# Eight early tiles of attention turned by TensorE in half precision instead of by DMA transposes, with a new issue order

## The chip, the cores and the metric

The kernel runs on one NeuronCore of a Trainium2 chip. A core has TensorE (PE, matrix products, writes to PSUM), VectorE (DVE), ScalarE (ACT), GpSimd (POOL) and SyncE (SP), each with a queue of its own that it works off in order, and 16 DMA engines that the queues feed; here SyncE issues all transfers. The metric is the device time of one execution in microseconds (us).

## The reference

```python
def _attn_ref(q, k, v, centroids):           # q, k, v: (4, 8, 768, 64); centroids: (8, 16, 64)
    q_assign = np.argmax(np.einsum('bhsd,hcd->bhsc', q_n, c_n), axis=-1)
    k_assign = np.argmax(np.einsum('bhsd,hcd->bhsc', k_n, c_n), axis=-1)
    mask = q_assign[:, :, :, None] == k_assign[:, :, None, :]
    scores = scale * np.matmul(q, k.transpose(0, 1, 3, 2))
    scores = np.where(mask, scores, -1000000000.0)
    attn = np.exp(scores - np.max(scores, axis=-1, keepdims=True))
    attn = attn / (np.sum(attn, axis=-1, keepdims=True) + 1e-09)
    return np.matmul(attn, v)

def _moe_ref(x, w1, w2, w3, w_out):          # x: (3072, 512); w1..w3: (512, 768); w_out: (768, 512)
    h = np.maximum(np.maximum(x @ w1, x @ w2), x @ w3)
    return h @ w_out
```

`q_n`, `k_n` and `c_n` are the rows divided by their norms. The output of attention, heads side by side, is the `x` of the feed-forward part. All inputs and outputs are float32. The kernel works with pairs of float16 numbers, a high half and a low half (the rest that the high half leaves), so that a product of two such numbers is three float16 products.

## The kernel before

**Tiles and stages.** There are 4 batches and 4 pairs of heads. A tile is 128 query rows of one head against all 768 keys. Each tile is a *step*; there are 192 steps, 48 to a batch. Three steps of each head of a pair (six steps) make a visit, and the visits go through a batch in two halves: the first three query blocks of all four pairs, then the last three. After 24 steps one half of a batch is complete, and its feed-forward part (`ffn`) can start: 18 groups of hidden products (`hid`, L1413) and three groups of output products (`outp`, L1468).

**A step** (`tile_units`): the score product (`pe`, L1256 and L1258, four matmuls into one of three `big` PSUM buffers), the row minimum with scaling on VectorE (`mx`, L1267), the exponential on ScalarE (`exp`, L1273), and then the tile is split into two float16 halves and turned so that keys lie on partitions, into `pt`. For batches after the first the tile is also divided by its row sums. There are two ways to turn it before the change. In steps 0, 2, 4 to 38 (`BY_PE`) TensorE transposes the float32 tile in six 128 x 128 blocks into a second `big` buffer (`ptr`, L1304), and the split happens on the way out of PSUM: the high half as a copy (L378 on ScalarE), the low half as a difference on VectorE (L1312). In all other steps the tile is split in SBUF: `hi` (a float16 copy, on ScalarE, GpSimd or VectorE), `lo` (the difference, L1279, on GpSimd or VectorE), both into `hl`; and one DMA transpose on SyncE's queue (`tr`, L1282) turns both halves at once into `pt`. Six turned tiles feed the product with the values (`av`, L1207, 36 matmuls).

**Preparation.** `prep` loads and splits the queries and keys of a pair and finds the clusters (among it L782 and L791, the cluster products of the first batch, and L548, a half-precision transpose of six blocks with its take L555), `v_prep` the values, `weights` the four weight matrices in pieces (`piece`: load, cast, L1030; `split16`: scale, high half, low half).

**What sets the order.** Every operation or short group is a unit of a plan; `ORDER` is a list of unit numbers written out in the source, and the units are issued in exactly that order, each to the queue of its engine. Where a unit may run on several engines, `HANDS` has a letter for it (V, S, G, Q for VectorE, ScalarE, GpSimd, SyncE). So the order of each engine's queue is fixed in the source. PSUM holds three `big` buffers (two banks each) and two `one` buffers (one bank each); the score tiles, the f32 transposes and the value products all share the three `big` ones, in the order of issue.

The names that matter below: `BY_PE`, `BY_16` (empty before the change), `hl`, `pt`, `big`, `HANDS`, `ORDER`, and `tile_units` with `ptr16` and `take16`, which stand in the source already but are used by no step before the change:

```python
        if step not in BY_16:
            u_t.append(add("SP", 1.43, tr, [u], [hl, pt], step, work=2.2))
            return
        o = big()
        def ptr16():
            d = o().bitcast(F16)
            for c in range(2 * QT):
                x = hl()[:, c // QT, c % QT * P : (c % QT + 1) * P]
                nc.tensor.transpose(d[:, c * P : (c + 1) * P], x, identh)
...
        u = add("PE", 0.85, ptr16, [u], [hl, o], step)
        for a in range(2):
            u_t.append(add({"ACT": 0.69, "DVE": 0.46}, 0, take16(a), [u], [o, pt], step))
```

Of the kernel before, what the change touches and what calls it, by code (L numbers as in the profile page):

```python
# [27 lines left out]
1 0 18 19 51 52 173 445 151 2-5 7 6 54 53 8-15 20 21 30 22-24 39 25 26 40 27 55 28 16 31 33 36 35 56 41 57 63  # L28
# [31 lines left out]
391-393 2645 1285 440 2646 2705 1289 1278 2638 1293 394 399 398 1290 463 2639 1301 467 441 1254 2647 2706 494  # L60
# [4 lines left out]
1296 534 507 1341 1297-1299 2650 480 536 509 1325 570 510 1355 508 1372 1356 512 537 1357 1300 1331 1332 513  # L65
# [5 lines left out]
2825 558 559 2674 1419 1402 1403 560 1404 1409 1434 2677 2676 1410-1412 2678 561 1420 562 487 1413 2765 1421  # L71
563-565 554 555 1396 628 1371 556 583 1405 566 1388 569 567 568 1426 2681 2683 1427 1414 577 2682 2679 1422
# [4 lines left out]
1507 1479 1470 1497 2699 1498 1508 1492 1483 1509 1460 2700 2702-2704 1510 1493 1461 1499 1511 1494 1462 1484  # L77
# [7 lines left out]
1602 1618 1610 1603 1625 2729 601 633 1626 2730 1611 605-607 2733 1633 1642 2735 2731 1619 1627 1628 1634 1643  # L85
# [1449 lines left out]
```

## Time and profile before

| | |
|---|---|
| median of 3 runs | 710.59 us (707.4 to 712.21) |
| profiled execution, time | 711.06 us |
| profiled execution, span from first to last instruction | 709.1 us |
| mean granted TensorE clock | 0.978 |
| DMA moved | 121.03 MB in 297795 packets, mean 171 GB/s |
| DMA transposes | 172, median 4.1 us from issue to landing |

The profile is one execution of the program on the chip. A row of a group gives line, engine, operation, output and inputs with their shapes, the count, then busy time and mean length in ns, then how long the engine stood idle just before these instructions and what ended that idle time. A row of the table by stages gives start and end of the stage, its length, and for each engine the busy time and, in brackets, the number of instructions; then the granted clock of TensorE as a share of full speed, the mean busy share of the 16 DMA engines and the rate. A row of the timeline gives start, length, engine, line, operation. Rows marked PEld are weight loads of TensorE, which overlap its products. The ends of matmuls are modelled.

### The profile page before, as it was taken

What the parts mean: (1) busy time and instruction counts of PE and PEld (TensorE: products, weight loads), DVE (VectorE), ACT (ScalarE), POOL (GpSimd) and SP (SyncE); (2) the same over time, 40 slices, a digit from 0 to 9 for tenths busy, and PEclk for the clock granted to TensorE, in tenths of its full rate; (3) what the DMA queues carried; (4) which work ended last, traced back from release to release, by engine and by line L of the source; (5) the groups of instructions that cost most, each with busy time, mean ns of one, the idle gap of its engine ahead of it and who ended that gap; (6) DMA issues with size and microseconds to landing.
All of it is one profiled execution on the core that took longest, in us unless ns stands there. A gap on an engine that the chain in (4) does not pass through costs nothing. (4 is left out here: it accounts for less than half of the span.)

```text
span 709.1 us, 13176 instructions
## 1 busy us (share of the span) xinstructions
PE 665.5 (94%) x4505; PEld 389.9 (55%) x4505; DVE 599.0 (84%) x1470; ACT 483.6 (68%) x841; POOL 403.3 (57%) x374
## 2 busy tenths in 40 slices
PE   3778778998999999999999999999999999999997
PEld 1554545555456655565555555655555646564663
DVE  7998999999998878999989888999899967784231
ACT  6988989989865657787767647786667775651000
POOL 3677887888656564857566545666584551531000
PEclk8578999999999999999999999999999999999999
DMA  6698878779798879998979998999999785775001
GB/s 225 199 216 182 207 210 205 188 174 202 168 196 188 172 126 217 197 185 195 215 156 194 179 189 181 185 196 196 197 194 178 145 164 112 148 158 125 1 1 60
DMA packets 297795, 121.03 MB, mean 171 GB/s; under 512 B 273024, under 2 KB 284160, under 8 KB 297728
## 3 DMA queue, kind: packets, MB, share of 16 engines
q1 hardware_dynamic: 297728, 120.20, 80.0%
q8 instruction: 35, 0.57, 0.3%
q14 instruction: 32, 0.26, 0.1%
HBM read 31.49 MB, written 6.29 MB: 53 GB/s over the span
## 5 line engine op out<-in xcount | busy, mean ns | idle before, releaser
L1267 DVE TENSOR_SCALAR_CACHE_REDUCE big<-big,nsc 128x768 f32<-128x768 f32 x192 | 192.7, 1016 | 11.4 <-PE big L1258 10.8
L1413 PE MATMUL one<-x,w16a 128*128 128x384 f16 x1152 | 197.0, 326 | 0.2
L1279 POOL TENSOR_TENSOR hl<-e,hl 128x768 f16<-128x768 f32 x86 | 144.4, 1682 | 61.1 <-ACT hl L378 34.2
L1413 PEld LDWEIGHTS <-w16a 128*128 128x128 f16 x1152 | 111.5, 98 | 75.7 <-issue 2.9
L1273 ACT ACTIVATE e<-big,nm 128x768 f32<-128x768 f32 x116 | 104.4, 901 | 49.7 <-DVE big L1267 32.3
L1256 PE MATMUL big<-qk 128*128 128x512 f16 (+1 forms) x384 | 96.6, 334 | 12.2 <-ACT e L1273 9.4
L1207 PE MATMUL big<-pt,v 128*64 128x384 f16 x1152 | 101.8, 330 | 2.4 <-ACT e L1273 1.4
L1413 PE MATMUL one<-x,w16b 128*128 128x384 f16 x576 | 98.9, 326 | 1.0 <-DVE worow L1098 1.0
L1258 PE MATMUL big<-qk 96*128 96x512 f16 (+1 forms) x384 | 96.1, 331 | 0.1
L1273 ACT ACTIVATE big<-big,nm 128x768 f32<-128x768 f32 x76 | 66.3, 872 | 43.7 <-DVE big L1267 35.3
L1207 PEld LDWEIGHTS <-v 128*64 128x64 f16 x1152 | 70.0, 111 | 33.2 <-issue 9.8
L1413 PEld LDWEIGHTS <-w16b 128*128 128x128 f16 x576 | 55.7, 98 | 40.1 <-issue 3.4
L1332 DVE SCALAR_TENSOR_TENSOR hl<-big,rs,hl 128x768 f16<-128x768 f32 x72 | 72.7, 1011 | 4.6 <-ACT hl L380 3.6
L380 ACT ACTIVATE hl<-big,rs 128x768 f16<-128x768 f32 x62 | 55.7, 898 | 27.3 <-issue 10.7
L1323 POOL TENSOR_SCALAR e<-e,rs 128x768 f32<-128x768 f32 x37 | 34.0, 919 | 65.9 <-DVE rs L1294 47.1
L1256 PEld LDWEIGHTS <-qk 128*128 128x128 f16 x384 | 35.3, 99 | 43.7 <-issue 22.1
L378 ACT CAST hl<-e 128x768 f16<-128x768 f32 x60 | 49.8, 831 | 5.3 <-POOL e L1323 4.5
L1258 PEld LDWEIGHTS <-qk 96*128 96x128 f16 x384 | 38.2, 100 | 27.1 <-issue 2.6
L818 POOL TENSOR_TENSOR qk<-stage,qk 128x768 f16<-128x768 f32 x26 | 43.8, 1686 | 9.2 <-ACT qk L378 5.5
L1468 PE MATMUL one<-wo,vf_h 128*128 128x512 f16 x216 | 48.3, 379 | 0.5 <-ACT o L380 0.4
L1468 PE MATMUL one<-wo,wf_h 128*128 128x512 f16 x216 | 48.3, 379 | 0.0
L1427 DVE SCALAR_TENSOR_TENSOR wf_h<-one,wf_h 128x384 f32<-128x384 f32 x48 | 26.5, 553 | 20.2 <-PE one L1413 19.6
(203 smaller groups left out, 1002.0 us busy)
## 6 DMA issues: line engine op xcount, KB each, us to landing
stage<-in_qk_dram SPq DMA_DIRECT2D x32, 384.0 KB, 4.3
wd<-in_moe_w_dram SPq DMA_DIRECT2D x18, 512.0 KB, 4.2
out_dram<-o SPq DMA_DIRECT2D x24, 256.0 KB, 2.9
qk<-qk SPq DMA_DIRECT2D x15, 384.0 KB, 4.3
qk<-qk SPq DMA_DIRECT2D x30, 192.0 KB, 3.5
stage<-in_v_dram SPq DMA_DIRECT2D x12, 384.0 KB, 4.0
wd<-in_moe_w_out_dram SPq DMA_DIRECT2D x6, 512.0 KB, 3.8
qk<-cl_t SPq DMA_DIRECT2D x60, 48.0 KB, 2.3
```

Source lines behind the costliest of these rows:

```text
L378: eng.copy(out, x)
L380: eng.activation(out, x, AF.Copy, scale=k)
L818: eng.tensor_tensor(t()[:, AQ, i], x(), t()[:, BQ, i], op=ALU.subtract)
L1207: nc.tensor.matmul(t()[D * i : D * i + D, 0:nb], v()[:, i, kt, a], pts[i % len(pts)]()[:, rows[i], c * QT + kt, :], start=(m == 0), stop=( ...
L1256: nc.tensor.matmul(t()[:, lo:hi], aq[:, qs], ak[:, lo:hi], start=True, stop=False)
L1258: nc.tensor.matmul(t()[:, lo:hi], bq[0:K2, qs], bk[0:K2, lo:hi], start=False, stop=True)
L1267: nc.vector.tensor_scalar(s, s, -SCALE if exact else nscs[:, b, pr : pr + 1], 3.0e38, op0=ALU.mult, op1=ALU.min, accum_out=nm())
L1273: nc.scalar.activation(e(), t()[:, 0:S], AF.Exp, bias=nm(), scale=-1.0, accum_out=r)
L1279: eng.tensor_tensor(hl()[:, 1, :], e(), hl()[:, 0, :], op=ALU.subtract)
L1332: eng.scalar_tensor_tensor(hl()[:, 1, :], e(), r(), hl()[:, 0, :], op0=ALU.mult, op1=ALU.subtract)
L1413: nc.tensor.matmul(t()[:, 0:nb], w16[jt // JA][:, jt % JA, wa, i, ct], x16[b, gi, ct]()[:, xa, 0:nb], start=(m == 0), stop=(m == 3 * CT - 1),)
L1468: nc.tensor.matmul(t()[:, 0:DM], h16(jt)[:, ha, tt * P : (tt + 1) * P], wo16[0][:, jt, wa, :], start=(m == 0), stop=(m == 3 * JT - 1),)
```

## The change

`BY_16` becomes the steps 1, 3, 5, 7, 9, 11, 13 and 15. These eight tiles are split in SBUF as before, and then TensorE transposes the two halves in twelve float16 blocks of 128 x 128 into a `big` PSUM buffer (seen there as float16), and two copies, one per half, take them to `pt`, each on ScalarE or VectorE. The DMA transposes of these steps fall away. With the steps 0, 2, 4 to 38, which went over TensorE before, the first 17 steps now need no DMA transpose. The plan has 3093 units instead of 3077 (eight times one TensorE unit and two takes more, one transfer less), so all numbers after the first such step shift, and `ORDER` and `HANDS` are replaced as a whole. No other line changes; line numbers after the order rise by one.

```diff
 ORDER = """
-1 0 18 19 51 52 173 445 151 2-5 7 6 54 53 8-15 20 21 30 22-24 39 25 26 40 27 55 28 16 31 33 36 35 56 41 57 63
...
+1 0 18 19 173 52 51 153 176 151 2-5 7 174 6 8-15 20 21 30 22 23 175 24 39 25 40 26 41 27 42 28 54 16 53 33 31
...
 HANDS = """
-VVSSSSSSVVSSSSSSGSGSGGQQGVSSGSGSVGQQGVSSSSGSSGQQGVSGGSVGSSGSSGGSGVSSGSSGSSGSSGVGSGSSGVSGSGGVVSGSGGSGGGGGVSGGSS
...
+VVSSSSVSVVVSSSSSGSGSGGQQGVSSSGGSGGQQGVVSGSGSGGQQGSGSGSSGSGGSGGGGGVSSGGGGSSGGGSVGSGVSGVGGSSGVSSGGGGSGGSSSVSSGSG
...
-    BY_16 = set()
+    BY_16 = set(range(1, 16, 2))
```

Counted over the whole order, VectorE has 1279 units instead of 1272, ScalarE 619 as before, GpSimd 348 instead of 339, TensorE 483 instead of 475 and SyncE 364 instead of 372. Of the sixteen takes eight are ScalarE's and eight VectorE's.

More of the change, by code (lines that the diff above doesn't have):

```diff
@@ L27 @@
 ORDER = """
-1 0 18 19 51 52 173 445 151 2-5 7 6 54 53 8-15 20 21 30 22-24 39 25 26 40 27 55 28 16 31 33 36 35 56 41 57 63
[31 rows of a table removed]
-391-393 2645 1285 440 2646 2705 1289 1278 2638 1293 394 399 398 1290 463 2639 1301 467 441 1254 2647 2706 494
[4 rows of a table removed]
-1296 534 507 1341 1297-1299 2650 480 536 509 1325 570 510 1355 508 1372 1356 512 537 1357 1300 1331 1332 513
[5 rows of a table removed]
-2825 558 559 2674 1419 1402 1403 560 1404 1409 1434 2677 2676 1410-1412 2678 561 1420 562 487 1413 2765 1421
-563-565 554 555 1396 628 1371 556 583 1405 566 1388 569 567 568 1426 2681 2683 1427 1414 577 2682 2679 1422
[4 rows of a table removed]
@@ L77 @@
-1507 1479 1470 1497 2699 1498 1508 1492 1483 1509 1460 2700 2702-2704 1510 1493 1461 1499 1511 1494 1462 1484
[7 rows of a table removed]
-1602 1618 1610 1603 1625 2729 601 633 1626 2730 1611 605-607 2733 1633 1642 2735 2731 1619 1627 1628 1634 1643
[8 rows of a table removed]
-1695 1723 1733 691 712 1741 2762 2763 619 1734 713 714 620 684 1742 2764 2768 1735-1737 1724 1725 695 621 1738
[12 rows of a table removed]
-1869 1870 2812 2946 1904 1839 1896 1871 1905 1872 1897 1873 1840 2814 1898-1900 1882 1891 1874 1912 2817 1913
-1914 2818 1906 1901 1929 2819 2821 1920 2815 1915 1916 1930 1917 1918 1907 1931-1933 1908 2816 2820 2822 1921
[10 rows of a table removed]
@@ L119 @@
-2071 2078 2859 2079 817 2091 2861 792 2092 818 819 2100 2080 820-822 2072 2860 793 2093 859 2862 2053 856 2064
[11 rows of a table removed]
-2900 893 2230 848 2231 2225 2237 2902 2245 918 913 914 2212-2214 877 2198 936 2215 2226 2905 2253 2907 2238
[11 rows of a table removed]
-945 2407 2396 3007 2367 2388 2950 2377 2368 2397 2408 2400-2402 3067 2409 2410 2952 2411 2415 2423 2424 2416
-2425 2954 2443 2412 2403 2417 2426 2404 2418 2419 2427 2413 2428 2420 2444 2445 2955 2378 2435 2379 2429 2421
-2380 2430 2446 2447 2436 2448 2437 2452 2957 2959 2469 2405 2422 2431 2414 2453 2438-2441 2470 2958 2471 2454
[9 rows of a table removed]
@@ L155 @@
-3010 3015 2596 3017 3019 3018 3020 3021 3025 3022-3024 3026 3027 3029 3028 3033 3030 3031 3034 3032 3035 3037
-3036 3041 3038-3040 3042 3043 3045 3044 3046-3049 3051 3050 3052 3053 3057 3054 3058 3055 3056 3059 3061 3060
-3062-3064 3068 3071 3069 3070 3016 3074 3072 3073 3075 3076
+1 0 18 19 173 52 51 153 176 151 2-5 7 174 6 8-15 20 21 30 22 23 175 24 39 25 40 26 41 27 42 28 54 16 53 33 31
[5 rows of a table added]
+182 981 1007-1009 166 142 201 993 1002 988 1003 982 183 184 1004 989 990 1013 1019 1010 185 1014 1015 126 1020
[10 rows of a table added]
@@ new lines @@
+230 1155 1136 1161 1156-1158 245 1137 246 1167 1162 247 231 1138 232 1163 248 1152 251 1171 1185 1168 233 249
[18 rows of a table added]
+1271 1351 1337 1343 531 1332 502 1272 1344 506 503 1338 1352 1310 532 473-475 2667 1296 535 466 1324 1333 478
[10 rows of a table added]
+569 628 1432 567 556 568 566 1441 583 1449 2842 1468 2706 1461 1469 1462-1464 1455 1465 2708 1470 1471 1423
+1456 1457 1424 1472 1473 1479 2709 1487 2713 1504 1474 1480 1488 1481 1489 1466 1458 1475 2669 2710 1490 1482
+1483 1491 1492 2711 1484 1505 1493 1485 2714 1506 2712 1494 2717 1496 1521 1507 1522 1497 1523 1498 1495 1486
@@ new lines @@
+1513 2715 1514 2716 1508 2718 1476 1515 2719 2720 1499 1509 1524-1526 1500 1516 1501 1502 1527 1510 1477 1528
+1511 1478 1517-1519 2724 1533 1541 1550 579 1534 1542 2725 1535 1543 1536 1551 1537 1544 1545 2783 1503 1512
[10 rows of a table added]
+680 1678 1679 1696 1639 1680 1688 1697 1681 1640 681-683 1698 1699 2762 685 1689 686 2763 2764 687 1690 1665
+604 616 708 617 1674 1682 1691 2767 1703 1712 2765 1704 1700 1705 688 2766 689 1701 1713 1714 1720 646 684
+1721 1706 650 1707 2768 1715 1716 690 651 1722 1717 2773 1737 2769 1729 1723 709 1724 652 653 710 1718 654-656
[9 rows of a table added]
@@ new lines @@
+1842 706 693 704 1810 694 707 705 735 732 1800 757 736 2809 758 759 763-765 729 740 1843 2810 1845 2811 1857
[3 rows of a table added]
+2820 2822 1891 1899 2827 2825 1900 1871 1892 1901 1893 2823 1872 1902 1903 1883 1894-1896 1884 1897 1904 2826
[8 rows of a table added]
+2032 2024 2013 2014 2037 2045 771 2858 2025 2038 2046 2033 2047 2048 2039-2041 2859 772 2061 2053 773-775 2054
[6 rows of a table added]
+2121 2883 825 2122 862 2135 2885 2127 2136 2113 2137 2886 2138 2128 863-865 2129 2130 2139 2131 801 798 2106
+799 800 797 2114 902 2123 2132 2884 2140 2141 2152 2887 2144 2889 2153 866 2133 2145 829 2154 2146 868 869 871
@@ L158 @@
+2142 872 2888 833 834 2147 2148 802 2890 2149 2891 2161 2895 2893 2169 870 803 2162 2155-2157 2894 2163 835
[3 rows of a table added]
+879 2194 2187 2201 880 2202 2203 2908 2177 2906 875 832 2188 2206 2215 2910 2207 2216 2217 2208 881-883 2218
[15 rows of a table added]
+2384 2413 2424 2425 2417 3083 2418 2419 2426 2427 2431 2439-2441 2970 2459 2432 2420 2968 2442 2433 2443 2434
[12 rows of a table added]
+3059 3061 3060 3062-3065 3067 3066 3068 3069 3073 3070-3072 3074 3075 3077 3076 3078-3080 3084 3087 3085 3032
+3090 3088 3089 3086 3091 3092
 """
 HANDS = """
-VVSSSSSSVVSSSSSSGSGSGGQQGVSSGSGSVGQQGVSSSSGSSGQQGVSGGSVGSSGSSGGSGVSSGSSGSSGSSGVGSGSSGVSGSGGVVSGSGGSGGGGGVSGGSS
@@ L162 @@
-GSSVSGSVSSGSSGSSGSGSVSSGGGGSSGGSSGSSSGSSGGSSGGGSSGGGSGSVSGGSSGQQGGVGSVSSSSGGGGQQGGVGSGSSVGGSSVQQGGVGSGSSGVGSSG
-QQVGVSGGSVGSGGSGQQVGVSGGVSSSGSVGQQGGVSSGVSGGGSSGQQGVVSSGSSSVGGGVQQGGVSSGSSGSGGSVQQVGVGSGSVSSGVSGQQVGVSSVSSGSGG
-SGQQGGVSSGSSGGGGSVQQGGVGSGSVGSGGSSGSGGSVGSSGSVGSSGSVGSSGSGGSSGSSGSSGSSVSSGSSGSSGSSGSSGSSGSSVSSGSSGSSGSSGSVSGSG
-GSVSVSVSGSVSGSVGSVSSGSVGGGSVSSGVSVSSGSVVSGSVGSGVSVSSGSVSVGSVGGVVSVGGGSVGSGSVGSGSSVGGGSVGSGSVSSGSVVGSVSVGGGSVSS
-GSSVGSGSVSGGVVSSGSSVSSGSVSGGSVGGGSSVVSGVVGVGSVSSGSSVGSGSVSSGSVGSGVSVGSGSVGSGVVSGGSSVVVGSVGGVSVGGGSVVGVGVVGSGSV
@@ L167 @@
-SGGVSVGGGSVGSGSVGSGVSVSGGSVSSGSVSSVSSVSGGSVSSGSVGVGSSVGSGSVGSGSVSGGSSVVSGSVGSGSVSGGSSVGGGSVSSGSVSSVSVVGVGSVGSG
-SVSSGSSVGSGSVSVGSVGSVSVVGGGSVGVGVVGSGVSVSSGSVGSGSVSVGVVVSGGSVSSGSVSGVSSVVVGSVVSGVVVSGSVVSVVVVGGSVVGGSVSVVVGVSV
-VSGSVVSGSVVVGVVVGGVVVVVSVSSVVVGSVVSGSVVSGSVVSGSVVVGSVVSGSSSVVVGGVVVSGVVVSGSVVSGSVVGGVVVGVSSVVVVSGSVVGGSVVGGVVV
-VGSVVSGSVVVVVSSVVVGGSVVGGSVVVGSVVGVSVVVVVVVGGSSSSVVSVSVVVVVVVSGSVVVVVVVVGSVVGVVVVVVVSVVVVSGVVVSVVVVGVSVVVVSVVV
-VVSS
+VVSSSSVSVVVSSSSSGSGSGGQQGVSSSGGSGGQQGVVSGSGSGGQQGSGSGSSGSGGSGGGGGVSSGGGGSSGGGSVGSGVSGVGGSSGVSSGGGGSGGSSSVSSGSG
@@ new lines @@
+GGSGGSSVSSGSSGSSGSSGVSGGGSGSSGGSGGSSSGGVGGSVSGSSSGSSGGSSSSVVSGQQVGVSSGSSSSGSGGQQGGVSSGSSGSGGSGQQGGVVSGSVGVGGSG
+QQGGVVGVSSGSGGSVQQGGVGVGSSGSGSVGQQGGVSSGVSGSGSSGQQGGVSVVSSGVGGVGQQVGVSGVSSGGGGSVQQGGVSGGSSSSGVSGQQGGVGGGVSSSGG
+SGQQGGVSVGVSGGGGSVQQGVVVSGSSGSSSGGSVSSGSSSSGSGGVSSSGVVSSVVVSSVVSGSVSSGVSSSGSSGVSGSSGSSGSGGVSGSSGVSGSSGSSGSSGSS
+GSSGSSGSSGSVSGSSGSVSVSVVGSVVGVGGVVSSGSVGSGSVSSGSSVSGGSVSSVVVVGGSSVSGGSVVGVVVGSGSSVGSVVVVSGVVSSGSSVGGVSVGVGVVGS
+GSSVGGGSVGGGSVSSGSSVSSGSVGVGSVSSVSSVGSGSVSSGSVSGGSSVSGGSVSSGSVSGGSSVSGGSVSSGSVGSGVSVGVGSVGSGSVGGVVSVGGGSVSVGSV
@@ L172 @@
+SSGSVVGSGVVGSGSVGSGSSVGGGSVGSGSVSGGVSVGGGSVSSGSVGGGSSVGGGSVSGGSVVSGSSVGSGSVGSGSVSSGSSVSSGSVGSGSVGSGSSVGGGSVSSG
+VVSGVSVVGSGVVSSGSVSSGSSVVGGVVSSGSVSSGSVVGSGSVVSGVVGGGSSVSSGVVVSGSVVGGSVVSSVVVSGGVVSGGSSVVSGVVVSGSVVSGSVVSGSVVS
+GSVVGGSSSSVVSGSVVVGSVVGGSVVVGSVVSGVVVSGSVSVVVGGSVVSGSVVGGSVVGGSVVGGVVVVGSSSSVVSVSVVSGVVVSGSVVGVSVVSGSVVGVVVSVV
+VSGSVVSGVVVSGSVVSGSVVSGSVVVVSSSSVVVGVVVGGVVVSGSVVSGSVVGGVVVGGSVSSVVSGSVVSVVVVSVSVVGVSVVGVVVVGGVSVSVVVGSVVVVVVV
+GVVVVVVSVVVVVVVVVVSS
 """
```

221 rows, old and new, of the table ORDER are left out of this document.

## The prediction, made before the changed kernel was run

> **What bounds the kernel now.** I read the head of the page first (span and busy shares), then the table by stages, then the groups and waits of one stage.
>
> ```profile
> span 709.1 us, 13176 instructions
> PE 665.5 (94%) x4505; PEld 389.9 (55%) x4505; DVE 599.0 (84%) x1470; ACT 483.6 (68%) x841; POOL 403.3 (57%) x374
> ...
> core 0: us, PE busy (x) PEld busy (x) DVE busy (x) ACT busy (x) POOL busy (x), PEclk, DMA share, GB/s
> 0.00:20.00 20.00, 6.77 (x25) 3.01 (x25) 15.51 (x48) 13.98 (x22) 6.81 (x38) 0.82 0.70 242
> 20.00:40.00 20.00, 16.86 (x88) 12.44 (x87) 19.64 (x44) 19.32 (x31) 13.78 (x11) 0.67 0.75 183
> 40.00:60.00 20.00, 16.44 (x101) 9.87 (x101) 16.84 (x35) 15.89 (x29) 15.72 (x11) 0.74 0.96 211
> 60.00:80.00 20.00, 15.66 (x132) 10.35 (x129) 18.83 (x39) 17.94 (x35) 16.03 (x14) 1.00 0.91 191
> 80.00:100.00 20.00, 13.14 (x105) 8.56 (x106) 19.54 (x36) 18.96 (x37) 17.32 (x15) 1.00 0.81 218
> 100.00:200.00 100.00, 92.91 (x679) 55.64 (x676) 98.00 (x238) 88.41 (x161) 78.58 (x72) 1.00 0.80 188
> 200.00:640.00 440.00, 438.50 (x2990) 254.51 (x2989) 389.72 (x999) 302.28 (x520) 252.26 (x213) 1.00 0.90 178
> ```
>
> The table splits the run in two. From 200 to 640 us TensorE (PE) is busy 438.50 of 440 us: there the time is TensorE's work and nothing else, and VectorE (DVE), ScalarE (ACT) and GpSimd (POOL) have room. Before 200 us it is the other way round. TensorE idles 13.23 us in the first 20 and 25.0 in the 180 after (3.14 + 3.56 + 4.34 + 6.86 + 7.09), while VectorE idles there 0.36 + 3.16 + 1.17 + 0.46 + 2.00 = 7.15 us. So the change, whose tiles all lie ahead of 100 us, works in the one part that TensorE does not fill, and the engine that has nothing to spare there is VectorE. ScalarE is next (18.96 of 20 at 80 to 100), GpSimd has most room, the DMA share is at its highest from 40 to 80 us.
>
> ```profile
> L1267 DVE TENSOR_SCALAR_CACHE_REDUCE big<-big,nsc 128x768 f32<-128x768 f32 x30 | 30.0, 1016 | 1.8 <-PE big L1258 1.6
> L1256 PE MATMUL big<-qk 128*128 128x512 f16 x64 | 18.3, 373 | 8.5 <-ACT e L1273 7.4 <-DVE pt L1312 0.8 <-DVE xs L1226 0.2
> L1304 PE MATMUL big<-ident,e 128*128 128x128 f32 x84 | 13.9, 309 | 4.7 <-ACT e L1273 3.7 <-DVE pt L1312 0.8
> ...
> L1279 POOL TENSOR_TENSOR hl<-e,hl 128x768 f16<-128x768 f32 x13 | 23.2, 1789 | 9.2 <-DVE hl L382 3.7 <-ACT hl L378 2.7 <-issue 1.9
> ```
>
> These are groups from 25 to 105 us. The score product (L1256) waits 7.4 us for the exponential of an earlier tile, which frees one of the three `big` PSUM buffers; the f32 transposes (L1304) wait 3.7 us for the exponential that makes their input. Neither waits for a transfer. L1279 is the split of a tile into its low half, most often on GpSimd.
>
> **The change part by part.** *Transfers taken away.* Eight of the 172 DMA transposes go, those of steps 1, 3 to 15.
>
> ```profile
> L1282 SPq DMA_TRANSPOSE pt<-hl x172: 1274/1561/3469, 35.1 to 648.3; - x172
> ...
> who waited for it (us, times):
>   POOL hl L382: 1.4, 2
>   ACT hl L378: 0.2, 1
> ```
>
> SyncE's queue loses 8 x 1.561 = 12.5 us of issuing, so loads queued behind them go out sooner. But in the whole run the engines waited only 1.4 + 0.2 = 1.6 us for these transfers. The gain is thus between 0 and 1.6 us by that row; I take 0 here, since both waits are GpSimd's and ScalarE's, and carry the relief of the DMA share as an unknown below.
>
> *TensorE.* Each tile now gets twelve 128 x 128 transposes in half precision. The trace has the same operation in L548, six blocks at once, once at the granted half clock and once at full:
>
> ```profile
> 33.54 0.82 PE L548 MATMUL one<-identh,cl_t 128*128 128x128 f16 x6 [1.69 <-DVE cl_t L543]
> ...
> 60.50 0.50 PE L548 MATMUL one<-identh,cl_t 128*128 128x128 f16 x6
> L548 PE MATMUL one<-identh,cl_t x12: 217/254/314, 33.5 to 60.8; 128*128 128x128 f16 x12
> ```
>
> At full clock six take 0.50 us, of which 0.25 is one block's length, so the step is 0.05 and twelve take 0.25 + 11 x 0.05 = 0.80; at half clock twice the 0.82, 1.64. Five tiles lie where the clock is partly halved, so 8 tiles cost 3 x 0.80 + 5 x 1.2 = 8.4 us (ends 6.4 and 13.1). All of it lies beside VectorE's work, in TensorE's 25.0 us of idle; I count 0. If that cover were gone, 8.4 us would be added in full. The group also brings a wait: it needs both halves of the split, so TensorE's queue can stand behind GpSimd's low half (1.789 us by L1279), with score products queued behind it, and VectorE and ScalarE wait for those. At worst that is 8 x 1.789 = 14.3 us, at best 0, if other work always stands between. The new order puts at least one score product between a tile's own and its f16 group, mostly two or three, and 25.0 - 8.4 = 16.6 us of idle lie above the worst; I take 0.
>
> The Trainium skill, page "VectorE: DVE Perf Modes", section "The three transpose paths", gives 390 ns for one 128 x 128 block on TensorE and 1309 ns by DMA; 96 blocks would then be an estimated 37.4 us, 12.4 more than TensorE's idle, and the time would be 710.6 + 12.4 = 723. The six blocks in 0.50 us above disagree: in a row they are pipelined, and the row decides.
>
> *The takes.* Each tile's result, twice 128 x 768 f16 in PSUM, is copied out by two new operations; the new hand string gives 8 to ScalarE and 8 to VectorE.
>
> ```profile
> L555 DVE TENSOR_SCALAR cl_t<-one,ksel x2: 578/594/610, 36.3 to 65.3; 128x768 f16<-128x768 f16 x2
> ...
> L378 ACT CAST pt<-big x20: 777/794/820, 33.3 to 143.9; 128x768 f16<-128x768 f32 x20
> ...
> L382 DVE TENSOR_SCALAR hl<-big,rs x10: 1000/1018/1020, 284.1 to 633.5; 128x768 f16<-128x768 f32 x10
> ```
>
> L555 reads the same f16 PSUM size: 8 x 0.594 = 4.75 us on VectorE (upper end by the f32 row, 8 x 1.018 = 8.1). ScalarE gets 8 x 0.794 = 6.4.
>
> *The new order and hands.* I counted what each engine's queue holds ahead of the score product of step 54, the point where TensorE has just become full:
>
> ```profile
> 193.07 0.50 PE L1256 MATMUL big<-qk 128*128 128x512 f16 x2
> ...
> 59.47 1.02 DVE L1267 TENSOR_SCALAR_CACHE_REDUCE big<-big,nsc 128x768 f32<-128x768 f32 x1 [0.26 <-PE big L1258]
> ...
> 60.42 0.14 DVE L1267 DVE_READ_ACCUMULATOR big<-big,nsc 128x1 f32 x1
> ```
>
> In both orders the same 136 TensorE units stand ahead of it (the new one has the 8 transposes besides), so what TensorE still has to do from there is the same. VectorE has 361 units ahead of it before and 370 after: the 8 f16 takes (4.75); 4 of the 20 takes of the f32-transposed tiles, which move from ScalarE (4 x 1.018 = 4.07 by the L382 row); and of the rest 9 come and 12 leave, each between 0.15 and 1.02 us by its own line's mean, 4.7 in and 6.8 out, net -2.1. Together 6.7. Neighbours on VectorE overlap by 0.07 us (59.47 + 1.02 against 60.42), 9 more of them take off 0.6: +6.1 us. ScalarE's balance is +1.0 (its 8 takes and 8 other pieces come, 14 leave), GpSimd's +4.7, which its idle covers: it was busy 78.58 of 100 us. SyncE has 10 units fewer ahead of that point: the eight transposes, and one `qk` move and one `v` load that go behind it. On TensorE the cluster products of pairs 2 and 3 go behind the first scores; both lie in its idle of the first 40 us, and I count them at 0.
>
> *The sum.* VectorE is the limit up to that point, so its +6.1 us goes to the end unless it idles less. Its 7.15 us of idle bound that relief: 0 to -7.15. I take half of the 3.16 at 40 to 60 us, where the DMA share is 0.96 and part of the removed transfers lay: -1.6. The profiled execution took 711.06 us, so 711.06 + 6.1 - 1.6 = 715.6; it lies 0.47 above the median of the runs shown, 710.59, so on their scale 715.1.
>
> **The rivals.** *PSUM (slower).* Each new tile takes one of three `big` buffers a second time. An f32 tile shows the hold:
>
> ```profile
> 59.19 0.82 PE L1304 MATMUL big<-ident,e 128*128 128x128 f32 x6
> ...
> 61.54 0.79 ACT L378 CAST pt<-big 128x768 f16<-128x768 f32 x1
> ...
> 62.36 0.96 DVE L1312 TENSOR_TENSOR pt<-big,pt 128x768 f16<-128x768 f32 x1
> ```
>
> From 59.19 to 63.32 it is 4.13 us, mostly waiting for busy ScalarE and VectorE. Eight such holds over three buffers are 11.0 us; at the least (0.80 + 0.79, the takes side by side) 4.2. If buffers decide, the stage grows by 11.0 instead of 4.5: 711.06 + 11.0 - 0.47 = 721.6. It decides from a hold of 4.5 x 3 / 8 = 1.7 us on if no buffer is ever free. The 7.4 us of waits of L1256 speak for it; against it, that these holds are long only because VectorE is late, so the two costs are largely one.
>
> *The clock (slower).* The granted clock is 0.67 and 0.74 from 20 to 60 us and 1.00 from then on. Should it stay at 0.74 for 60 to 100 as well, TensorE's 28.8 us of work there would be 38.9, 10.1 more against 11.2 of idle; if none of that idle can be used, 715.1 + 10.1 = 725. The Trainium skill, "TensorE: Matmul & The Clock Gate", "Part 4: PE-mode transpose", says that transposes do not count as activity for the gate, which would bring this about; no run here shows it, and at 60 to 100 us the trace keeps the full clock with f32 transposes in between.
>
> *A chain, not VectorE, limits the first part (faster).* If what holds TensorE is the way from score to transposed tile, the new order may halve what is left of its 25.0 us after the 8.4 of new work: 711.06 - 8.3 - 0.47 = 702.3. For it: the waits for the exponential, and a DMA share of 0.96. Against it: VectorE at 98.00 of 100 us.
>
> *Nothing changes.* The transfers were hidden, the extra VectorE work is not needed by then and slides past 200 us, where it has 50 us of room: 710.6.
>
> **How the numbers follow.** VectorE's load: 0.50, its own range from full relief (711.06 + 6.1 - 7.15 - 0.47 = 709.5) to the case that the pieces handed on save nothing (715.1 + 1.6 + 2.1 = 718.8). PSUM 0.20, clock 0.05, chain 0.14, nothing 0.11. Within 1% (703.5 to 717.7, about what a measurement of this kernel can tell from no change) lie four fifths of the first case, all of the last and crumbs of the others: 0.56. Slower: 0.09 of the first, 0.17 of PSUM, 0.05: 0.31. Faster: 0.13. The range 704.5 to 722 cuts off most of the chain case and the upper part of the two slower ones, some 2 in 10.
>
> **What would show it.** VectorE's busy time over the first 200 us at 188 of 200 or more, and the score product of step 54 near 198 instead of 193 us, with TensorE's idle of the first 200 us down by a few us only. Each f16 group at 0.8 to 1.6 us and a VectorE take near 0.59 would confirm the prices. A rise of L1256's waits for the exponential or for `pt` well above 8 us in 25 to 105 us would show PSUM; a clock below 1 after 60 us the clock. I am wrong if step 54 comes at or before 193 us, or if TensorE is no longer full from 200 us on.

## The result, and the profile after

| | before | changed |
|---|---|---|
| median of 3 runs | 710.59 us | 721.98 us (718.83 to 722.88) |
| profiled execution: time, span | 711.06, 709.1 us | 718.83, 717.0 us |
| score product of step 54 starts (profiled execution) | 193.07 us | 199.38 us |

The changed kernel is slower: its time is 1.0143 of the time before, 95% interval 1.0095 to 1.0191. A second measurement gave 720.44 us and 1.0130 (1.0102 to 1.0157). The forecast of 715.1 is 1.0064 of 710.59 and lies below both intervals; 721.98 lies at the upper end of the range given (722.0).

The head of the page and the table by stages of the changed kernel, with the columns as before:

```profile
span 717.0 us, 13344 instructions
...
PE 672.1 (94%) x4601; PEld 395.5 (55%) x4601; DVE 605.6 (84%) x1477; ACT 478.2 (67%) x841; POOL 408.8 (57%) x383
```

```profile
0.00:20.00 20.00, 7.36 (x21) 2.14 (x21) 15.86 (x44) 12.55 (x20) 5.76 (x37) 1.00 0.75 258
20.00:40.00 20.00, 14.50 (x66) 10.88 (x66) 17.56 (x40) 15.17 (x25) 12.69 (x12) 1.00 0.54 159
40.00:60.00 20.00, 16.50 (x163) 12.30 (x163) 18.55 (x39) 17.35 (x30) 18.48 (x13) 1.00 0.48 134
60.00:80.00 20.00, 14.97 (x132) 10.80 (x133) 19.06 (x32) 17.22 (x31) 14.87 (x14) 0.91 0.48 127
80.00:100.00 20.00, 15.22 (x131) 9.72 (x128) 19.39 (x39) 16.97 (x34) 16.35 (x13) 1.00 0.59 139
100.00:200.00 100.00, 93.86 (x679) 56.11 (x676) 97.54 (x241) 93.24 (x168) 80.80 (x72) 0.97 0.82 186
200.00:640.00 440.00, 436.55 (x2975) 253.32 (x2974) 390.06 (x996) 297.15 (x522) 251.64 (x217) 1.00 0.92 177
```

The DMA share at 40 to 60 us has halved, from 0.96 to 0.48, and the time got no better for it. VectorE was busy 187.96 of the first 200 us, as before (188.36). TensorE's idle in 20 to 200 us is 24.95 us, again as before (25.0), although it now also does the transposes. From 200 to 640 us TensorE is idle 3.45 us instead of 1.50 in these two profiles: a smaller loss of up to 2 us, which the prediction did not have. Most of the loss is there by step 54 (+6.3 of the +7.8 between the two profiled executions).

The groups that belong to the change, first from 25 to 105 us (busy time, mean ns, idle time before them and what ended it), then the takes' own rows (shortest, median, longest ns):

```profile
L1257 PE MATMUL big<-qk 128*128 128x512 f16 x27 | 11.9, 441 | 7.7 <-ACT e L1274 3.7 <-DVE pt L1313 3.5 <-ACT pt L1358 0.2
...
L1350 PE MATMUL big<-identh,hl 128*128 128x128 f16 x96 | 7.5, 230 | 2.8 <-ACT pt L379 1.5 <-ACT e L1274 0.9 <-DVE pt L1313 0.2
```

```profile
L1358 ACT COPY pt<-big x8: 790/802/825, 43.4 to 86.3; 128x768 f16<-128x768 f16 x8
```

```profile
L1360 DVE COPY pt<-big x8: 547/549/558, 45.3 to 85.3; 128x768 f16<-128x768 f16 x8
```

The 96 blocks took 7.5 us of TensorE together; the takes 8 x 0.549 = 4.4 us on VectorE and 8 x 0.802 = 6.4 us on ScalarE. The score product waited 7.7 us for a buffer, before 8.5, but over 27 products instead of 32, and for something else: waits for an exponential fell from 7.4 to 3.7 us, and waits for VectorE's take of an f32-turned tile (L1312 before, L1313 now) rose from 0.8 to 3.5. In after_again, the second profile of this kernel, the whole is 9.1 us, and 4.6 of them are for that take. The f16 takes themselves (L1358) account for 0.2 and 0.6 us.

What each engine did ahead of step 54's score product is the sum on which the prediction rested. One row for before, one for the changed kernel:

```profile
0.00:193.07 193.07, 155.61 (x1082) 96.68 (x1082) 181.50 (x418) 171.29 (x303) 143.73 (x153) 0.92 0.80 197
```

```profile
0.00:199.38 199.38, 161.79 (x1179) 101.64 (x1179) 187.48 (x429) 172.49 (x304) 148.33 (x157) 0.97 0.70 174
```

VectorE worked 187.48 - 181.50 = 6.0 us more and idled 199.38 - 187.48 = 11.9 us instead of 11.6. But TensorE also worked 6.2 us more and idled as long as before (37.6 and 37.5 us). The same two rows therefore allow two causes, VectorE's added work and TensorE's, and a third: the order itself was longer, and the added work merely fitted into it. The runs had to tell these apart.

### The profile page after: what moved, and what is told of

Its sections match the earlier page's. It is cut to its first block, busy times and chain, and to the rows that moved or that the text cites. A ratio compares the mean times of both kernels' runs of the same rounds, so it can differ in the third digit from the quotient of the medians.

```text
span 717.0 us, 13344 instructions
## 1 busy us (share of the span) xinstructions
PE 672.1 (94%) x4601; PEld 395.5 (55%) x4601; DVE 605.6 (84%) x1477; ACT 478.2 (67%) x841; POOL 408.8 (57%) x383
## 5 line engine op out<-in xcount | busy, mean ns | idle before, releaser
L1208 PE MATMUL big<-pt,v 128*64 128x384 f16 x1152 | 100.3, 327 | 1.9 <-ACT e L1274 1.3
L381 ACT ACTIVATE hl<-big,rs 128x768 f16<-128x768 f32 x54 | 48.3, 899 | 22.2 <-issue 11.3
L379 ACT CAST hl<-e 128x768 f16<-128x768 f32 x62 | 51.3, 828 | 12.2 <-POOL e L1324 8.4
L1324 POOL TENSOR_SCALAR e<-e,rs 128x768 f32<-128x768 f32 x31 | 28.8, 928 | 41.8 <-DVE rs L1295 36.0
L1428 DVE SCALAR_TENSOR_TENSOR wf_h<-one,wf_h 128x384 f32<-128x384 f32 x48 | 26.5, 553 | 21.2 <-PE one L1414 19.6
```

The source lines that it names most:

```text
L379: eng.copy(out, x)
L381: eng.activation(out, x, AF.Copy, scale=k)
L1208: nc.tensor.matmul(t()[D * i : D * i + D, 0:nb], v()[:, i, kt, a], pts[i % len(pts)]()[:, rows[i], c * QT + kt, :], start=(m == 0), stop=( ...
```

## The experiments

My theory after the result was the prediction's own: VectorE limits the part ahead of step 54, and its 6 us more are the loss. The rivals: the f16 groups on TensorE, the takes on ScalarE and VectorE as a chain, and the new order by itself. All runs were timed against the kernel before on the same chip; ratios are with 95% intervals.

| run | median, us | before, us | ratio | interval |
|---|---|---|---|---|
| after_again | 720.44 | 711.17 | 1.0130 | 1.0102 to 1.0157 |
| new_order_transfers | 727.38 | 711.17 | 1.0219 | 1.0193 to 1.0245 |
| old_order_f16 | 723.63 | 711.17 | 1.0193 | 1.0158 to 1.0228 |
| old_order_vector_load | 717.14 | 711.17 | 1.0078 | 1.0056 to 1.0099 |
| new_takes_on_scalar | 722.20 | 710.34 | 1.0168 | 1.0152 to 1.0183 |
| new_all_on_scalar | 731.50 | 710.34 | 1.0280 | 1.0258 to 1.0302 |
| old_order_scalar_load | 715.73 | 710.34 | 1.0079 | 1.0064 to 1.0094 |
| old_order_vector_load_late | 714.53 | 710.34 | 1.0055 | 1.0036 to 1.0075 |
| new_order_no_takes | 717.88 | 712.33 | 1.0066 | 1.0040 to 1.0091 |
| new_order_no_turn | 718.40 | 712.33 | 1.0083 | 1.0054 to 1.0112 |
| old_order_no_turn | 710.71 | 712.33 | 0.9983 | 0.9956 to 1.0011 |
| new_order_alone | 719.08 | 712.40 | 1.0086 | 1.0058 to 1.0114 |

### The change measured once more, and its two parts apart

**after_again** is the changed kernel without an edit. 

> The changed kernel once more, to narrow its ratio and to have a second profile of it on the chip of the other runs. All theories: 716 to 723 us; the score product of step 54 near 199 us, against 193 us in the kernel before.

**new_order_transfers** has the changed order, but the eight tiles go by DMA transpose again, each at the place of its f16 group:

```diff
-    BY_16 = set(range(1, 16, 2))
+    BY_16 = set()
 ORDER: each ptr16 unit of steps 1, 3 to 15 becomes the tr unit of that step, the takes go
```

> The new order and hands, but the eight tiles go over DMA transposes again: each f16 group is replaced in the order by one transfer, the sixteen takes fall away. If VectorE's load is what costs (the first theory), 8 x 0.55 = 4.4 us of VectorE work go, and the time is 4 to 5 us under the changed kernel, about 716 to 717. If PSUM holds cost (the second), eight holds go and the time falls by up to 11, to about 711. If the new order costs whatever turns the tiles (the third), the time stays at 720 to 723.

**old_order_f16** has the order before, with the f16 groups and their takes (one on ScalarE, one on VectorE) put in soon after each low half:

```diff
-    BY_16 = set()
+    BY_16 = set(range(1, 16, 2))
 ORDER: each tr unit of these steps goes; ptr16 and two takes are put in from 6 units after lo on
```

> The order and hands of before, with the f16 turning put in: for each of the eight tiles the TensorE group and its two takes (one on ScalarE, one on VectorE) stand at the first place after the tile's low half at which a PSUM buffer is free. By VectorE's load 4.4 us more than before, 715; by PSUM up to 11 more, 718 to 722, the more so as nothing else was moved to make room; by the third theory (the new order costs) 711 to 713.

**old_order_vector_load** is the kernel before with eight VectorE reductions whose result nobody uses:

```diff
+        if step in EXTRA:                      # steps 1, 3 to 15, after lo
+            add("DVE", 0.5, extra, [u_cw], [], step)
...
+        nc.vector.tensor_reduce(junk, x, axis=AX.X, op=ALU.max)
```

> The kernel before with eight extra VectorE reductions over 384 f16 constants, 0.55 us each by a like row, one behind the low half of each of steps 1 to 15; nothing reads them, they wait for nothing and take no PSUM. By VectorE's load 4.4 us more than before, 715, and step 54 near 197; by PSUM or by the new order, 710 to 712.

Neither of the two mixed kernels separated the parts cleanly. In new_order_transfers the waits of TensorE from 55 to 75 us show a new one, larger than all others:

```profile
PE big L1256 <- DMA qk<-qk: 9.7, 1, 9.7
```

That `qk` move is issued by SyncE, whose queue now holds the transposes ahead of it; the order was made for tiles that do not use SyncE. So 1.0219 is the time of this stall and of the order together. In old_order_f16 the turning, put into an order that has no place for it, cost 12.5 us: step 54 came at 204.71 us, with 185.1 us of VectorE's work ahead of it and 19.6 us of idle. That is less work than in the changed kernel and more idle, the first sign that VectorE's work alone is not the measure. old_order_vector_load seemed to speak for the theory: 8 x 0.546 = 4.4 us of added work cost 6.0 us.

### Is it VectorE?

If it is, work taken off VectorE must bring time back, and the same work on ScalarE, or on VectorE after 200 us, must be nearly free. **new_takes_on_scalar** and **new_all_on_scalar** only change letters of the changed kernel:

```diff
 HANDS, take16 of steps 3 to 15 (eight units):  V -> S
 HANDS, f32 take of steps 12, 18, 24, 28:       V -> S     (second kernel only)
```

> The changed kernel with the eight f16 takes that VectorE did (0.549 us each) given to ScalarE; nothing else differs. VectorE's load as the cause: VectorE has 8 x 0.549 = 4.4 us less ahead of the score product of step 54, which comes some 4 us earlier than the 199.4 to 202.1 us of the changed kernel, and the time falls from about 720.5 to about 716. A chain through ScalarE as the cause: ScalarE gets 8 x 0.802 = 6.4 us more and both takes of a tile run one after the other, so step 54 comes later by up to 6 us and the time is 721 to 727. The order alone as the cause (what stands where, not who does it): no change, 719 to 722.

> As the run before it, and the four copies of f32-turned tiles (steps 12, 18, 24, 28) that the change moved from ScalarE to VectorE go back to ScalarE as well (4 x 1.018 = 4.07 us off VectorE). VectorE's load as the cause: VectorE holds about 8.5 us less than in the changed kernel, step 54 comes at about 193 us and the time is about 712. ScalarE as the next limit: it has 6.4 + 4 x 0.794 = 9.6 us more than in the changed kernel, so most of the gain is lost and the time stays at 716 to 722. The order alone: 719 to 722.

**old_order_scalar_load** and **old_order_vector_load_late** add work to the kernel before:

```diff
+            add("ACT", 0.5, extra, [u_cw], [], step)     # steps 1, 3 to 15: three copies of 128 x 8
...
+    EXTRA = set(range(81, 96, 2))                        # the VectorE reductions, 294 to 346 us
```

> The kernel before with 24 small copies added on ScalarE (three after the low half of each odd step from 1 to 15, about 0.2 us each, 4.8 us in all); they compute nothing that is used. It is the counterpart of the run that added 8 x 0.546 us on VectorE and came out 6 us slower. VectorE's load as the cause: ScalarE has idle of its own there, so 0 to 1.5 us, 711 to 712.5. Any added work in the early queues costs its length (the order is tight on every engine): 4 to 7 us, 715 to 718.

> The kernel before with the same eight extra VectorE reductions of 0.546 us as in the earlier run, but after the low half of each odd step from 81 to 95, that is past 200 us, where TensorE is full and VectorE has some 50 us of room. VectorE's load ahead of the point where TensorE becomes full as the cause: 0 to +1 us, 711 to 712. A disturbed order, or any work on VectorE, as the cause: +4 to +6 us, 715 to 717.

All four went against the theory. The row ahead of step 54 in new_takes_on_scalar:

```profile
0.00:203.88 203.88, 163.78 (x1178) 104.45 (x1178) 183.75 (x421) 178.05 (x312) 148.69 (x157) 0.92 0.70 170
```

VectorE had 187.48 - 183.75 = 3.7 us less to do, and step 54 came at 203.88 us, later than in either profile of the changed kernel (199.38, and 202.08 in after_again): VectorE's idle grew to 20.1 us. With four more takes moved, the time rose to 1.0280. ScalarE's added copies were

```profile
L521 ACT COPY junk<-cw x8: 183/196/217, 34.7 to 69.8; 128x8 f16<-128x8 f16 x8
L522 ACT COPY junk<-cw x8: 197/197/198, 34.9 to 70.1; 128x8 f16<-128x8 f16 x8
L523 ACT COPY junk<-cw x8: 197/197/198, 35.1 to 70.3; 128x8 f16<-128x8 f16 x8
```

4.7 us together, and cost 5.4 us by the medians, nearly as much as VectorE's 6.0, though ScalarE idled 21.8 us ahead of step 54 in the kernel before. The profiled executions of the two runs differ more: step 54 came at 200.29 us with the work on VectorE (the slowest execution of its run) and at 195.82 us with the work on ScalarE (the fastest of its run), 7.2 and 2.8 us later than before. Past 200 us, where VectorE has 50 us of room, eight reductions still cost 4.2 us by the medians. In the profiled execution of that run (712.0 us, near its fastest) TensorE idled 2.19 us in the stage that holds them, against 0.81 in the kernel before and 1.3 to 1.5 in the other four profiles with its order. So this trace shows 0.7 to 1.4 us of the cost; where the rest lies is not shown:

```profile
200.00:400.00 200.00, 197.81 (x1356) 114.43 (x1354) 181.03 (x469) 137.19 (x235) 122.22 (x101) 1.00 0.93 184
```

So an engine's idle, summed over a stage, is not slack for work put in at a given place. The theory that VectorE alone limits the first part fell; what I put in its place, argued and not shown, was that the queues are fitted to each other piece by piece.

### The order without the turning

Three kernels leave the turning of the eight tiles out; in place of the takes or transposes one transfer per tile puts constants into `pt`. **new_order_no_takes** keeps the f16 groups, **new_order_no_turn** does not, **old_order_no_turn** is the kernel before without its eight transposes.

```diff
-        for a in range(2):
-            u_t.append(add({"ACT": 0.69, "DVE": 0.46}, 0, take16(a), [u], [o, pt], step))
+        u_t += [u, add("SP", 0.6, fill, [], [pt], step, work=2.0)]
```

> The changed kernel with its order and its eight f16 groups on TensorE, but without the sixteen takes; in their place one plain transfer per tile puts constants into the tile's part of the transposed buffer, which waits for no engine's work. The output is not the reference's: the eight tiles are left out of it. It asks which part of the change costs the 10 us. The takes (work on VectorE and ScalarE) as the cause: 4.4 us less on VectorE and 6.4 us less on ScalarE, 712 to 716. The f16 groups on TensorE as the cause: 718 to 721. The new order and its hands as the cause: 718 to 721 here and in the next run as well.

> As the run before it, and without the f16 groups on TensorE (8 x 0.83 = 6.6 us): the new order and hands alone, with plain transfers of constants where the takes stood; the eight tiles are left out of the result. The takes as the cause: the same as the run before it within 1.5 us, 711 to 716. The groups as the cause: 712 to 715, some 6 us below the run before it. The order and hands as the cause: 718 to 721.

> The kernel before with its eight early DMA transposes replaced by the same plain transfers of constants, at the places of the transposes; the eight tiles are left out of the result. It bounds what the transposes could have cost, whatever takes their place. The prediction's row (the engines waited 1.6 us for transposes in the whole run): 709 to 711. The transposes held the first part up: 703 to 707.

**new_order_alone** does without those transfers too: for the first three visits the product with `v` reads one tile's part of `pt` three times.

```diff
-                        pts[i % len(pts)]()[:, rows[i], c * QT + kt, :],
+                        pts[i]()[:, i : i + 1, c * QT + kt, :].broadcast_to([P, gn, P])
+                        if begin[n] < 16
+                        else pts[i % len(pts)]()[:, rows[i], c * QT + kt, :],
```

> The changed kernel with its order and hands, but without the f16 groups, without the takes and without any transfer in their place; the products with v read a neighbouring tile's part of the transposed buffer instead, so the eight tiles are left out of the result. The two runs before it put transfers of constants there, which raised the DMA share at 40 to 60 us from 0.48 to 0.78, and one of them then waited 3.6 us for a qk move; this run has no such transfers. The work that turns the tiles (takes 4.4 us on VectorE and 6.4 us on ScalarE, groups 6.6 us on TensorE) as the whole cause: 710 to 713. The order and hands as the whole cause: 719 to 721, and the score product of step 54 at 199 us or later. Both, in the shares of VectorE's queue (4.4 of the 6.0 us from the takes): 715 to 717, step 54 at about 195 us.

The table of these runs beside the others, as ratios to the kernel before:

| | not turned at all | by transfers | by f16 groups |
|---|---|---|---|
| order before | 0.9983 | 1 | 1.0193 |
| new order | 1.0086 | 1.0219 (SyncE stall) | 1.0130 and 1.0143 |

The new order with its hands costs 6.1 to 6.7 us with nothing turned (0.0086 x 711; 719.08 - 712.40). With the f16 groups and without the takes it is no slower (1.0066; 1.0083 without the groups), so the groups cost nothing that can be measured. The whole turning adds 0.0044 to 0.0077 to the order-only runs, 3.1 to 5.5 us; the intervals overlap for two of the three, and in the profiled executions the spans of the changed kernel and of new_order_no_takes differ by 1.3 us only (717.0 and 715.7).

The rows of new_order_alone, up to step 54 and then between the score products of steps 12 and 18, the latter with the same passage in the kernel before and in the changed one (the profiled execution of new_order_alone, 720.76 us, is the slowest of its six):

```profile
0.00:201.05 201.05, 161.04 (x1083) 97.31 (x1083) 184.40 (x421) 167.28 (x296) 147.25 (x157) 0.87 0.70 173
62.90:83.90 21.00, 16.41 (x109) 9.87 (x107) 16.49 (x27) 16.91 (x31) 15.89 (x14) 0.76 0.38 106
```

```profile
59.80:73.40 13.60, 10.69 (x93) 7.01 (x92) 13.33 (x25) 11.60 (x23) 10.02 (x10) 1.00 0.90 184
```

```profile
62.80:82.00 19.20, 16.16 (x144) 11.82 (x144) 18.05 (x32) 18.17 (x33) 14.50 (x12) 0.92 0.47 127
```

Without the takes VectorE has 184.40 us of work ahead of step 54, 3.1 less than the changed kernel, and 16.65 us of idle, 4.8 more. It does not use the place that the takes left. In new_order_no_takes it is the same: 183.09 us of work, 16.3 us of idle, and step 54 at 199.41 us, as in the changed kernel. In the passage from step 12 to 18 the kernel before fills VectorE to 13.33 of 13.60 us; the new order has more pieces there on every engine (31 instead of 23 on ScalarE, 14 instead of 10 on GpSimd) and fills none: VectorE 16.49 of 21.00. (Step 19's score product also stands in this passage in the new order; by that of step 24 the distance to the kernel before is 6.5 us in the changed kernel and 8.2 in new_order_alone, instead of 8.6 and 10.6 by step 18.) What VectorE waits for in that passage are the others in turn:

```profile
DVE xs L1228 <- PE big L1207: 2.2, 1, 2.2
DVE xs L1228 <- POOL hl L1281: 2.0, 1, 2.0
```

In the changed kernel the takes fill this room (18.05 of 19.20). So the new order holds a place for the takes, and the place costs its time whether they stand in it or not. This reading is argued from the rows, and the table adds that the same turning costs 0.0193 in the order before, which has no such place. Why the room had to be as large as 6 us, and whether a third order could hold the takes for less, was not tried and stays open.

The same rows leave a rival open, the clock. Ahead of step 54 new_order_alone has the matrix products of the kernel before (x1083 and x1082), but TensorE was busy 161.04 us with them instead of 155.61, at a granted clock of 0.87 instead of 0.92. Of the 8.0 us by which its step 54 came later, 5.4 are longer busy time and 2.6 idle. In new_order_no_turn, also without the groups, they are 3.6 of 6.2 us (159.16 busy, step 54 at 199.27). In the first profile of the changed kernel, TensorE's 6.2 us more are less than the 7.5 us of its f16 groups. So the split of the loss into order and turning is one of times; whether the order costs them by its places, or in part by the lower clock that comes with it, no run separates.

## Why the prediction was right or wrong

The range, 704.5 to 722, holds the first measurement by 0.02 us, and that is luck: 721.98 lies where the PSUM and clock rivals had their sums, and the likeliest case, a time within 1% of the one before (0.56), did not come. The signs named for VectorE came (187.96 of 200 us busy, step 54 at 199.38 us), but a longer order gives them as well, so they could not show VectorE as the cause.

*Transfers taken away, 0.* Right. old_order_no_turn leaves the transposes out (a plain transfer stands at each place) for 0.9983 (0.9956 to 1.0011), so in the order before, no other way of turning these eight tiles could be expected to gain more than some 3 us.

*TensorE, 8.4 us, hidden.* Right in size and in effect, though TensorE's idle did not shrink by it (24.95 us against 25.0). The groups took 7.5 us of busy time, 78 ns for each of 96 blocks, which overlap (one lasts 230 ns), and the order is no faster without them. The Trainium skill, "VectorE: DVE Perf Modes", "The three transpose paths", gives 390 ns for a block; the measurement differs. The time that the prediction worked out from it, 723, lies near the result, but by a cost that is not there.

*The takes.* The sizes were right, 0.549 us on VectorE (0.594 forecast) and 0.802 us on ScalarE (0.794). As a price the turning came to 3.1 to 5.5 us, against 4.75.

*The new order and hands.* The step that failed. The count of VectorE's queue gave +6.1 us ahead of step 54, and the trace shows +6.0. But the conclusion drawn from it, "VectorE is the limit up to that point, so its +6.1 us goes to the end unless it idles less", does not hold as a cause: with 3.1, 3.7 and 4.4 us of that work taken away (new_order_alone, new_takes_on_scalar, new_order_no_takes), VectorE idles 4.8, 8.2 and 4.4 us longer, and step 54 comes at 201.05, 203.88 and 199.41 us, against 199.38 and 202.08 in the two profiles of the changed kernel. Without the f16 takes the count leaves 4.07 - 2.1 = 2.0 us for the order and hands; they cost 6.1 us (719.08 - 712.40 = 6.7 by the medians). That term was mis-sized by 4 us: the pieces were counted on one queue and not by where they stand among the others.

One such place was counted at 0, the cluster products that go behind the first scores. One set of 24 of them moved from 17 to 24 us (first two rows) to 31 to 36 us (third row), and VectorE, which had not waited for it before, then waited 2.3 us:

```profile
16.90 0.61 PE L791 MATMUL one<-cwn,stage 128*128 128x32 f32 x2 [3.49 <-DMA stage<-in_qk_dram]
19.22 4.91 PE L791 MATMUL one<-cwn,stage 128*128 128x32 f32 x22 [1.72 <-DMA stage<-in_qk_dram]
```

```profile
30.59 5.17 PE L792 MATMUL one<-cwn,stage 128*128 128x32 f32 x24
```

```profile
DVE cl_m L528 <- PE one L792: 2.3, 1, 2.3
```

This wait stands in all eight profiles with the new order and in none of the six with the order before. How much of it reaches the end is not shown; step 12's score product came 3.0 us later (62.8 instead of 59.8).

*The relief, -1.6.* Wrong. VectorE idled 0.3 us more ahead of step 54 (1.7 in after_again). In the stage it was taken from, 40 to 60 us, VectorE's idle did fall, from 3.16 to 1.45 us, with the DMA share at 0.48; but from 20 to 40 us it rose from 0.36 to 2.44 us, by the wait for the cluster products, and nothing was left of it. With 0 in its place the forecast would have been 716.7.

*After 200 us, 0.* Missed, by a little. From 200 to 640 us TensorE idles 2.5 to 3.7 us in the eight profiles with the new order (3.67 in new_order_alone), and 1.5 to 2.9 in the six with the order before, of which the profile shown ahead of the prediction is the lowest. So about 1 us may belong to the order.

*The rivals.* PSUM's sum, 721.6, is close to the time, but its sign, waits of the score product for the exponential or for `pt` well above 8 us, did not come: they were 8.2 us before and are 7.4 and 8.9 in the two profiles of the changed kernel. The part for `pt` did rise (from 0.8 to 3.7 and 5.2 us), but the order costs its 6 us in new_order_no_turn and new_order_alone too, where the eight tiles take no second buffer. The chain rival and "nothing changes" are excluded by both intervals. The clock rival was given 0.05, and its sign, a clock below 1 after 60 us, came: at 60 to 80 us the granted clock was 1.00 in all six profiles with the order before, and 0.74 to 0.91 in all eight with the new one. It comes in stretches of 3 to 10 us at half speed (62.6 to 66.0 us in the first profile of the changed kernel, 74.4 to 81.2 in after_again, 71.1 to 81.3 in new_order_alone). Two executions of the changed kernel suggest a price. Rows for 60 to 66 and 72 to 80 us, of the first and of after_again:

```profile
60.00:66.00 6.00, 3.99 (x27) 2.87 (x27) 5.64 (x10) 3.96 (x8) 4.45 (x7) 0.72 0.35 104
72.00:80.00 8.00, 6.21 (x62) 4.42 (x62) 7.53 (x12) 7.32 (x13) 7.00 (x6) 1.00 0.75 203
```

```profile
60.00:66.00 6.00, 3.13 (x31) 2.26 (x31) 6.00 (x12) 3.72 (x8) 4.45 (x6) 1.00 0.39 111
72.00:80.00 8.00, 6.33 (x36) 3.66 (x36) 6.33 (x10) 6.47 (x11) 6.98 (x6) 0.65 0.72 205
```

Step 15's score product began at 71.8 us in both; step 18's at 82.0 in the first and 84.6 in the second, which had the slow stretch just there. In 72 to 80 us TensorE was as busy in both but got through 36 matmuls instead of 62, and VectorE lost 1.2 us. So where such a stretch falls may be worth up to 2.6 us; this rests on one pair of executions. What it is worth for the order itself is the open point above. The Trainium skill, "TensorE: Matmul & The Clock Gate", "Part 4: PE-mode transpose", would make the f16 transposes the reason, since by it they do not count as activity. The runs speak against that: new_order_alone has none of the f16 transposes and the lower clock at 60 to 80 us (0.76, against 0.91 and 0.86 in the two profiles of the changed kernel).

## What to carry to other kernels

When a change brings a new order with it, time that order with the new work left out before any of the work is priced: here the order, with its hands, made some two thirds of the loss. A queue that is busy 98% of a stage looks like the limit, but the test is to take work off it: if its idle grows by as much, it was not the limit by itself. Here 4.4 to 4.7 us of added pieces cost 4 to 6 us on either of two engines, and past 200 us too, where VectorE has 50 us of room. And before replacing an operation, leave it out once: eight transfers whose absence gains nothing that can be measured cannot pay for what is put in their place.

## What the runs showed of the hardware

- The column of the granted clock can show full speed where there was none. Between 20 and 40 us it shows 1.00 in the first profile of the changed kernel and 0.50 in after_again (the row below), but the score products took the same in both, 0.83 to 0.85 us for two at 27 to 37 us, against 0.48 to 0.49 at 42 to 47 us (rows of the first profile, then of after_again). So TensorE was equally slow there in both, and step 15 began at 71.8 us in both.

```profile
20.00:40.00 20.00, 14.27 (x59) 10.66 (x59) 17.53 (x42) 15.01 (x24) 12.69 (x12) 0.50 0.54 155
```

```profile
27.25 0.84 PE L1257 MATMUL big<-qk 128*128 128x512 f16 x2
42.34 0.49 PE L1257 MATMUL big<-qk 128*128 128x512 f16 x2
```

```profile
27.48 0.85 PE L1257 MATMUL big<-qk 128*128 128x512 f16 x2
43.21 0.49 PE L1257 MATMUL big<-qk 128*128 128x512 f16 x2
```

- The clock fell without a long pause of TensorE. In after_again it went to half speed at 74.4 us; in the 12 us before, the longest pause between two matmuls was 1.2 us. But TensorE was busy only 8.28 of these 12.4 us:

```profile
62.00:74.40 12.40, 8.28 (x76) 5.73 (x75) 12.23 (x22) 12.09 (x23) 7.44 (x8) 1.00 0.40 113
74.40:81.20 6.80, 6.04 (x34) 3.54 (x36) 5.13 (x8) 4.93 (x8) 6.36 (x5) 0.50 0.55 152
```

- A VectorE take of 128 x 768 f16 out of PSUM took 0.549 us, and one of 128 x 768 f32 in the same stage (L383) 0.940 us. On ScalarE they took 0.802 and 0.797 us (L379), so there the type made no difference.
